# Loading w_down in sixteen 8-partition transfers in a streaming decode kernel

## The chip, the core and the metric

The kernel runs on one core of a Trainium2 chip. The metric is the device time of one execution in microseconds, taken as the median over several executions; less is better. The profile shown here is one further execution, recorded by the hardware profiler.

## What is computed

One decode step of a gated mix of two branches, for one token x of width 512. Branch A is grouped-query attention over a cache of 32768 positions (32 query heads, 8 key/value heads, head width 128) with its query and output projections. Branch B is a SwiGLU feed-forward layer of width 1792. A sigmoid gate mixes them.

```python
def _A_ref(x, k_cache, v_cache, wq, wo):
    q = (x @ wq).reshape(B, Sq, Hq, Dh).transpose(0, 2, 1, 3)
    k = jnp.repeat(k_cache, rep, axis=1)
    v = jnp.repeat(v_cache, rep, axis=1)
    p = _softmax(jnp.einsum("bhqd,bhkd->bhqk", q, k) * (Dh ** -0.5))
    o = jnp.einsum("bhqk,bhkd->bhqd", p, v)
    return o.transpose(0, 2, 1, 3).reshape(B, Sq, Hq * Dh) @ wo

def _B_ref(x, w_gate, w_up, w_down):
    return (_silu(x @ w_gate) * (x @ w_up)) @ w_down

g = _sigmoid((x * gate_w).sum(-1, keepdims=True))
return g * _A_ref(...) + (1 - g) * _B_ref(...)
```

All inputs are bfloat16. The two caches are 64 MB each; the weights wq, w_gate, w_up, w_down and wo come to about 14 MB. Every byte is read once.

## The kernel before

**The stream.** A list named `stream` (L65 to L71) has 35 entries, numbered 0 to 34, and gives the order of all large loads: "Q" (wq), two K entries of group 0, "F" (w_gate and w_up), then K of group g and V of group g-1 in turn for both halves of the cache, the last two V entries, and "O" (wo). A K or V entry is half of one group's cache, 16384 positions: 128 partitions of 32768 bytes, 4 MB. Each partition holds 128 consecutive positions.

**Pages.** SBUF holds five pages of 4 MB (`page`, NPG = 5). Entry i uses page i mod 5. Besides these there is a buffer of its own for w_down: `wd`, 128 partitions of 14 x 512 bfloat16, 14336 bytes in each partition.

**The queue that issues.** SyncE (SP) walks through the stream (L259 to L288). For entry i of 5 or more it first waits until TensorE has released entry i-5 (L261), then it issues the transfer. So at most five entries are issued and not yet released. w_gate, w_up and, right behind them, w_down are issued with entry 3 ("F", L268 to L274). wo is cut into five transfers along its rows (`WO_CUTS`, L276 to L279). All these transfers go through one DMA queue, q1, which the sixteen DMA engines serve; every transfer adds 16 to its semaphore when it has landed. ScalarE issues only the two small loads of x and gate_w (L463, L464).

**What uses the data.** TensorE takes the entries in the same order (L428 to L442). For a K entry it transposes 128 blocks (`emit_fill`, L346), VectorE copies them to SBUF (L578), and TensorE forms the scores (L364). For a V entry it waits for the exponentials of ScalarE and accumulates `ps_o` (L386). Right before entry 32, the V entry of group 7 and half 0, `emit_ffn_out` (L412) waits for w_down and multiplies with it. After the last V entry come the normalisation, the products with wo in five parts as these land (L451 to L454), a transpose of the result and the store of 4 x 128 elements (L290).

The lines that the change touches are L269 to L274 (the "F" branch of SP's loop) and L414 (the wait for w_down).

Of the kernel before, what the change touches and what calls it, by code (L numbers as in the profile page):

```python
# [13 lines left out]
def bass_gated_mix__gqa_block_cached__swiglu_ffn__decode_kernel(  # L14
# [24 lines left out]
    FC = F // 128  # L39
# [20 lines left out]
    assert KC * H * DH <= PAGE and 2 * KC * F <= PAGE and WOJ * NOUT <= PAGE  # L60
    WO_CUTS = [0, 16, 24, 28, 30, 32]
    OC = NOUT // 128


    stream = [("Q",), ("K", 0, 0), ("K", 0, 1), ("F",)]  # L65
# [7 lines left out]
    with ExitStack() as es:  # L73
        def S_(name):
            return es.enter_context(nc.semaphore(name))
# [4 lines left out]
        sem_ld_wd = S_("s_ld_wd")  # L80
# [39 lines left out]
        def T(name, shape, dt):  # L120
            return es.enter_context(nc.sbuf_tensor(name, shape, dt))
# [23 lines left out]
        wd = T("wd", [128, FC, NOUT], BF16)  # L145
# [13 lines left out]
        O2 = T("O2", [128, WOJ], BF16)  # L159
        res_col = T("res_col", [128, OC], BF16)  # L160
        res_row = T("res_row", [OC, 128], BF16)

# [18 lines left out]
        def cache_view(i):  # L181
            return page[:, i % NPG, :].rearrange("p (r d) -> p r d", d=DH)
# [28 lines left out]
        with nc.Block("main") as block:  # L211
# [45 lines left out]
            @block.sync  # L257
            def _(sp):
                for i, e in enumerate(stream):  # L259
                    if i >= NPG:  # L260
                        sp.wait_ge(*freed[i - NPG])  # L261
                    sem = sem_page[i % NPG]
                    if e[0] == "Q":
                        sp.dma_start(wq_v, A_wq.rearrange("(p c) n -> p c n", c=KC)).then_inc(  # L264
                            sem, 16
                        )
                    elif e[0] == "F":
                        for w, src in enumerate((B_w_gate, B_w_up)):  # L268
                            sp.dma_start(  # L269
                                wgu[:, w, :, :], src.rearrange("(p c) f -> p c f", c=KC)  # L270
                            ).then_inc(sem, 16)
                        sp.dma_start(
                            wd[:, :, :], B_w_down.rearrange("(p j) n -> p j n", j=FC)
                        ).then_inc(sem_ld_wd, 16)  # L274
                    elif e[0] == "O":
                        src = A_wo.rearrange("(p j) n -> p j n", j=WOJ)  # L276
                        for k, s in enumerate(sem_wo):
                            a, b = WO_CUTS[k], WO_CUTS[k + 1]
                            sp.dma_start(wo_v[:, a:b, :], src[:, a:b, :]).then_inc(s, 16)  # L279
                    else:  # L280
                        cache = A_k_cache if e[0] == "K" else A_v_cache
                        _k, g, b = e
                        sp.dma_start(
                            cache_view(i),
                            cache[0, g, b * BLK : (b + 1) * BLK, :].rearrange(
                                "(p r) d -> p r d", r=R
                            ),
                        ).then_inc(sem, 16)  # L288
                sp.wait_ge(sem_dve_row, 1)
                sp.dma_start(  # L290
                    out[0, 0, :].rearrange("(c n) -> c n", c=OC), res_row[:, :]
                ).then_inc(sem_out, 16)
                sp.wait_ge(sem_out, 16)

            @block.tensor
            def _(pe):
# [103 lines left out]
                def emit_proj(w, vec, j, first, last):  # L400
                    for oc in range(OC):
                        ins = pe.matmul(  # L402
                            ps_c[:, oc : oc + 1],
                            w[:, j, oc * 128 : (oc + 1) * 128],
                            vec[:, j : j + 1],
                            start=first and oc == 0,
                            stop=last,
                            skip_group_check=True,
                        )
                    return ins  # L410

                def emit_ffn_out():  # L412
                    pe.wait_ge(sem_dve_tT, 1)
                    pe.wait_ge(sem_ld_wd, 16)  # L414
                    for j in range(FC):
                        emit_proj(wd, tT, j, j == 0, False)

# [10 lines left out]
                for i, e in enumerate(stream):  # L428
                    if e == ("V", G - 1, 0):
                        emit_ffn_out()  # L430
                    elif e == ("V", G - 1, NB - 1):
                        emit_sums()
                    if e[0] != "O":
                        pe.wait_ge(*landed[i])
                    if e[0] == "Q":
                        emit_q()
                    elif e[0] == "F":
                        emit_ffn()
                    elif e[0] == "K":
                        emit_k(i)  # L440
                    elif e[0] == "V":
                        emit_v(i, e[1], e[2])  # L442
# [8 lines left out]
                for k, s in enumerate(sem_wo):  # L451
# [5 lines left out]
                pe.matmul(  # L457
                    ps_r[0:OC, 0:128], res_col[:, :], ident[:, :], start=True, stop=True
                ).then_inc(sem_pe_fin, 1)
# [41 lines left out]
            def _(dve):  # L501
# [104 lines left out]
                dve.wait_ge(sem_pe_sum, 1)  # L606
                dve.tensor_copy(res_col[:, :], ps_c[:, 0:OC]).then_inc(sem_dve_res, 1)  # L607
                dve.wait_ge(sem_pe_fin, 1)
# [29 lines left out]
```

## Time and profile before

| | |
|---|---|
| time, median of 3 runs (lowest to highest) | 361.88 us (361.78 to 361.90) |
| the profiled execution's own time | 361.94 us |
| its span in the profile | 360.1 us |
| TensorE matmul, busy | 273.6 us (76% of the span) |
| VectorE, busy | 185.3 us (51%) |
| ScalarE, busy | 30.4 us (8%) |
| moved by DMA | 148.99 MB in 5972 packets, mean 414 GB/s |
| issue of w_down on SP | at 3.16 us, takes 0.45 us |
| products with w_down on TensorE | 336.4 to 337.9 us |
| five issues of wo on SP | 317.21 to 319.44 us |
| issue of the result's store on SP | at 358.50 us |

The span runs from the first to the last recorded instruction; the run's own time is 1.84 us longer. Times inside the profile count from the span's start. A line such as L283 is a line of the kernel before. A page of the profile gives busy times, the span in 40 slices, the DMA queues, the chain of work that ended last, groups of instructions, and the transfers with their times from issue to landing. Beside what is printed, the trace keeps a record of each DMA packet (start, duration, bytes, queue) and of each step of a semaphore that a landing transfer raises, so that a transfer on sixteen engines leaves sixteen landing times.

### The profile page before, as it was taken

What the parts mean: (1) busy time and instruction counts of PE and PEld (TensorE: products, weight loads), DVE (VectorE), ACT (ScalarE), POOL (GpSimd) and SP (SyncE); (2) the same over time, 40 slices, a digit from 0 to 9 for tenths busy, and PEclk for the clock granted to TensorE, in tenths of its full rate; (3) what the DMA queues carried; (4) which work ended last, traced back from release to release, by engine and by line L of the source; (5) the groups of instructions that cost most, each with busy time, mean ns of one, the idle gap of its engine ahead of it and who ended that gap; (6) DMA issues with size and microseconds to landing.
All of it is one profiled execution on the core that took longest, in us unless ns stands there. A gap on an engine that the chain in (4) does not pass through costs nothing.

```text
span 360.1 us, 14005 instructions
## 1 busy us (share of the span) xinstructions
PE 273.6 (76%) x6580; PEld 269.4 (75%) x6580; DVE 185.3 (51%) x305; ACT 30.4 (8%) x142; POOL 4.6 (1%) x19
## 2 busy tenths in 40 slices
PE   0339988958696968969796969799696959697474
PEld 0339988958696968969796969799596859697474
DVE  0218935829292845738291937557282917566001
ACT  1000001500400030000300030001200030001100
POOL 0000000000000000000000000000000000000000
PEclk9999976959587785959695877859596956878555
DMA  8999999999999999999999999999999999999972
GB/s 335 422 439 402 441 422 435 431 419 435 424 426 442 421 415 439 424 433 428 414 440 424 420 442 417 422 439 419 439 428 420 435 424 420 440 420 430 423 302 101
DMA packets 5972, 148.99 MB, mean 414 GB/s; under 512 B 666, under 2 KB 668, under 8 KB 1052
## 3 DMA queue, kind: packets, MB, share of 16 engines
q1 hardware_dynamic: 5912, 148.12, 96.4%
q8 instruction: 51, 0.84, 0.9%
q14 instruction: 5, 0.04, 0.0%
q10 hardware_dynamic: 4, 0.00, 0.0%
HBM read 148.11 MB, written 0.00 MB: 411 GB/s over the span
## 4 chain that ended last, share of the span: by engine, by line
DMA 51%; PE 40%; issue 7%; SPq 1%; another core or an unknown queue 0%; DVE 0%
DMA page<-in_A_k_cache_dram 40%; PE pst L346 24%; DMA page<-in_A_wo_dram 11%; PE ps_sc L364 8%; PE ps_o L386 7%; PE ps_m L329 2%; SPq L279 0%; PE pst L402 0%; SPq L264 0%; PE pst L457 0%; DVE res_row L609 0%; DVE res_col L607 0%
## 5 line engine op out<-in xcount | busy, mean ns | idle before, releaser
L578 DVE COPY ktT<-pst 128x1024 bf16<-128x1024 bf16 x256 | 168.7, 691 | 119.0 <-PE pst L346 118.7
L346 PE MATMUL pst<-ident,page 128*128 128x128 bf16 x2048 | 179.3, 245 | 18.4 <-DMA page<-in_A_k_cache_dram 16.1
L346 PEld LDWEIGHTS pst<-ident,page 128*128 128x128 bf16 x2048 | 143.6, 111 | 19.8 <-issue 10.0
L386 PE MATMUL ps_o<-ET,page 128*128 128x4 bf16 x2048 | 65.0, 168 | 44.6 <-issue 42.2
L364 PE MATMUL ps_sc<-qT,ktT 128*128 128x4 bf16 x2048 | 90.2, 165 | 5.7 <-issue 5.1
L386 PEld LDWEIGHTS ps_o<-ET,page 128*128 128x128 bf16 x2048 | 59.7, 100 | 45.9 <-issue 43.3
L364 PEld LDWEIGHTS ps_sc<-qT,ktT 128*128 128x128 bf16 x2048 | 80.2, 98 | 6.6 <-issue 5.7
L476 ACT ACTIVATE nbias<-gmax 128x4 f32<-128x4 f32 x8 | 1.6, 206 | 279.9 <-POOL gmax L253 279.9
L486 ACT ACTIVATE ET<-ps_sc,nbias 128x128 bf16<-128x128 f32 x64 | 22.5, 377 | 0.4 <-ACT nbias L476 0.2
L566 DVE TENSOR_REDUCE pmaxf<-ps_sc 128x4 f32<-128x512 f32 x16 | 11.0, 690 | 13.3 <-PE ps_sc L364 13.3
L486 ACT ACTIVATION_READ_ACCUMULATOR ET<-ps_sc,nbias 128x1 f32 x64 | 13.8, 216 | 0.0
L315 PE MATMUL ps_m<-xT,page 128*128 128x1 bf16 x128 | 3.6, 165 | 5.3 <-DMA page<-in_A_wq_dram 5.3
L315 PEld LDWEIGHTS ps_m<-xT,page 128*128 128x128 bf16 x128 | 3.5, 104 | 5.4 <-issue 5.4
L329 PE MATMUL ps_m<-xT,page 128*128 128x1 bf16 x112 | 6.9, 198 | 0.0
L253 POOL PARTITION_ALL_REDUCE gmax<-pmax x8 | 3.0, 374 | 303.3 <-DVE pmax L570 303.3
L329 PEld LDWEIGHTS ps_m<-xT,page 128*128 128x128 bf16 x112 | 6.8, 168 | 0.0
L302 PE MATMUL ps_m<-ones_bf,x_row 1*128 1x1 bf16 x4 | 0.3, 171 | 7.8 <-DMA gw_row<-in_gate_w_dram 7.8
L302 PEld LDWEIGHTS ps_m<-ones_bf,x_row 1*128 1x128 bf16 x4 | 0.2, 112 | 7.8 <-DMA gw_row<-in_gate_w_dram 7.8
L594 DVE RECIPROCAL rS<-pst 128x32 f32<-128x32 f32 x1 | 0.4, 358 | 10.1 <-PE pst L420 10.1
L402 PE MATMUL pst<-O,page 128*128 128x1 bf16 x128 | 4.0, 166 | 1.8 <-issue 1.1
L402 PEld LDWEIGHTS pst<-O,page 128*128 128x128 bf16 x128 | 3.7, 105 | 2.1 <-issue 1.2
L503 DVE CAST xT<-ps_m 128x4 bf16<-128x4 f32 x1 | 0.2, 161 | 8.3 <-PE ps_m L302 8.3
(48 smaller groups left out, 18.5 us busy)
## 6 DMA issues: line engine op xcount, KB each, us to landing
page<-in_A_k_cache_dram SPq DMA_DIRECT2D x16, 4096.0 KB, 40.1
page<-in_A_v_cache_dram SPq DMA_DIRECT2D x16, 4096.0 KB, 37.9
page<-in_A_wq_dram SPq DMA_DIRECT2D x1, 4096.0 KB, 12.7
page<-in_A_wo_dram SPq DMA_DIRECT2D x1, 2048.0 KB, 34.9
page<-in_B_w_gate_dram SPq DMA_DIRECT2D x1, 1792.0 KB, 35.9
page<-in_B_w_up_dram SPq DMA_DIRECT2D x1, 1792.0 KB, 39.7
wd<-in_B_w_down_dram SPq DMA_DIRECT2D x1, 1792.0 KB, 43.5
page<-in_A_wo_dram SPq DMA_DIRECT2D x1, 1024.0 KB, 37.1
```

The costliest lines, as they stand in the source:

```text
L253: pool.partition_all_reduce(gmax[:, g, :], pmax[:, g, :], 128, ReduceOp.max).then_inc(sem_gmax, 1)
L302: ins = pe.matmul(ps_m[:, base + c : base + c + 1], srcv[:, c, :], ones_bf[0:1, 0:1], start=True, stop=True,)
L315: ins = pe.matmul(ps_m[:, M_Q0 + h : M_Q0 + h + 1], wq_v[:, c, h * DH : (h + 1) * DH], xT[:, c : c + 1], start=(c == 0), stop=(c == KC - 1),)
L329: ins = pe.matmul(ps_m[:, base + j : base + j + 1], wgu[:, w, c, :].rearrange("d (p j) -> d j p", j=FC)[:, j, :], xT[:, c : c + 1], start= ...
L346: ins = pe.transpose(pst[j % NST][:, t * 128 : (t + 1) * 128], view[:, q * TPF + t, :], ident[:, :],)
L364: ins = pe.matmul(ps_sc[f % NSC][:, col : col + HPG], ktT[:, j % NKT, t * 128 : (t + 1) * 128], qT[:, g * HPG : (g + 1) * HPG], start=True ...
L386: ins = pe.matmul(ps_o[:, g * HPG : (g + 1) * HPG], view[:, r, :], ET[:, g % NEG, :, n], start=(n == 0), stop=(n == NT - 1),)
L402: ins = pe.matmul(ps_c[:, oc : oc + 1], w[:, j, oc * 128 : (oc + 1) * 128], vec[:, j : j + 1], start=first and oc == 0, stop=last, skip_gr ...
L476: act.activation(nbias[:, g, :], gmax[:, g, :], ACT.Copy, scale=-SCALE).then_inc(sem_nbias, 1)
L486: act.activation(ET[:, g % NEG, h, b * R : (b + 1) * R], sc[:, h, :], ACT.Exp, bias=nbias[:, g, h : h + 1], scale=SCALE, accum_out=esum[:, ...
L566: dve.tensor_reduce(pmaxf[:, f, :], sc, AX.X, ALU.max).then_inc(sem_pmax, 1)
L578: dve.tensor_copy(ktT[:, j % NKT, :], pst[j % NST][:, :]).then_inc(sem_cp, 1)
```

## The change

w_down is no longer loaded behind w_up by one transfer. It is cut along its partitions into 16 transfers of 8 partitions each; the c-th is issued with entry 8 + c of the stream (entries 8 to 23), after SP's wait for the free page and right before that entry's own transfer. All sixteen raise the same semaphore, and the wait ahead of the products with w_down is for 256 in place of 16. Sources, destinations and the bytes that are loaded are the same.

```diff
+    WD_P = 8
+    WD_N = 128 // WD_P
+    WD_AT = 8
...
                     sem = sem_page[i % NPG]
+                    if 0 <= i - WD_AT < WD_N:
+                        p = (i - WD_AT) * WD_P
+                        sp.dma_start(
+                            wd[p : p + WD_P, :, :],
+                            B_w_down.rearrange("(p j) n -> p j n", j=FC)[p : p + WD_P, :, :],
+                        ).then_inc(sem_ld_wd, 16)
...
-                        sp.dma_start(
-                            wd[:, :, :], B_w_down.rearrange("(p j) n -> p j n", j=FC)
-                        ).then_inc(sem_ld_wd, 16)
...
-                    pe.wait_ge(sem_ld_wd, 16)
+                    pe.wait_ge(sem_ld_wd, 16 * WD_N)
```

## The prediction

> **What bounds the kernel now.** I read the page's slices first, to see which resource is full and where it stops being full.
>
> ```profile
> PE   0339988958696968969796969799696959697474
> DMA  8999999999999999999999999999999999999972
> GB/s 335 422 439 402 441 422 435 431 419 435 424 426 442 421 415 439 424 433 428 414 440 424 420 442 417 422 439 419 439 428 420 435 424 420 440 420 430 423 302 101
> ```
>
> DMA is full in every slice from the second to the 38th, at about 428 GB/s, while TensorE has gaps nearly everywhere. The two last slices, 9 us each, run at 302 and 101 GB/s. The chain of work that ended last names TensorE for much of the span, but only because SP's issues wait for released pages:
>
> ```profile
> DMA 51%; PE 40%; issue 7%; SPq 1%; another core or an unknown queue 0%; DVE 0%
> ...
> page<-in_A_k_cache_dram SPq DMA_DIRECT2D x16, 4096.0 KB, 40.1
> page<-in_A_v_cache_dram SPq DMA_DIRECT2D x16, 4096.0 KB, 37.9
> ...
> wd<-in_B_w_down_dram SPq DMA_DIRECT2D x1, 1792.0 KB, 43.5
> ```
>
> A 4 MB page at 428 GB/s needs 9.8 us, yet lands 38 to 40 us after its issue: it stands behind three other pages. A later issue costs nothing as long as that queue holds some 28 us of work. So the end is set by the DMA engines emptying the queue. Then the queues, and the end of the stream in windows (the last three columns are granted clock, DMA share and GB/s):
>
> ```profile
> DMA packets 5972, 148.99 MB, mean 414 GB/s; under 512 B 666, under 2 KB 668, under 8 KB 1052
> ...
> q1 hardware_dynamic: 5912, 148.12, 96.4%
> q8 instruction: 51, 0.84, 0.9%
> ...
> q10 hardware_dynamic: 4, 0.00, 0.0%
> ```
>
> ```profile
> 340.00:345.00 5.00, 3.37 (x107) 3.28 (x106) 0.00 (x0) 0.00 (x0) 0.00 (x0) 0.50 0.98 411
> 345.00:350.00 5.00, 2.59 (x96) 2.55 (x96) 0.60 (x2) 0.00 (x0) 0.00 (x0) 0.50 0.69 282
> 350.00:355.00 5.00, 2.82 (x93) 2.58 (x91) 0.60 (x3) 0.00 (x0) 0.00 (x0) 0.50 0.50 200
> 355.00:360.10 5.10, 2.64 (x82) 2.29 (x78) 0.44 (x2) 0.00 (x0) 0.00 (x0) 0.50 0.07 24
> ```
>
> The share falls to exactly one half: eight of sixteen engines are done while eight still work. The landing records say it engine by engine: the last part of wo lands on six engines at 346.2 to 347.2 us, on a seventh at 348.2, on an eighth at 351.2, and on the other eight at 355.5 to 357.2. For the first transfer, wq, the sixteen lay within 0.9 us. The gap grows evenly: some engine falls back by about 1.56 us whenever it serves a packet of q8, and the packet records show 48 of the 51 packets going round eight engines, six to each (6 x 1.56 = 9.4 us). I call these the late eight and the others the early eight. TensorE's last products start at 357.26 us, right behind the last of the late eight.
>
> **The change, part by part.** q1's packets took 96.4% of 16 x 360.1 us, 5554 engine-us for 148.12 MB: 26.7 KB per us and engine, so a row of w_down (14336 B) takes 0.54 us.
>
> *Removed:* one transfer of 128 rows, 8 rows for each engine: 8 x 0.54 = 4.3 us off all sixteen. The issues agree: w_up lands at 2.67 + 39.7 = 42.4 us, w_down at 3.16 + 43.5 = 46.7.
>
> *Moved earlier:* entry 4 and what follows land up to 4.3 us sooner until entry 8. It is worth nothing at the end, since the same bytes still go through the queue; the products with w_down at 336.4 us stand some 80 us behind the last piece.
>
> *Added on SP:* 15 more issues. With the neighbouring rows at 0.33 us (a page) and 0.45 (w_down), each delays its entry by at most 0.45 us, hidden by the 28 us of queue; without that cover it would be 16 x 0.45 = 7.2 us. No new wait is queued: the pieces stand behind a wait that SP had anyway.
>
> *Added on the engines.* On how many engines does a transfer of 8 partitions run? The counts tell: 41 transfers of 128 partitions with one semaphore packet from each of 16 engines are 41 x 144 = 5904 of q1's 5912 packets; 8 are left for the result's store, whose four rows thus had four semaphore packets, not sixteen: four engines. q10 has 4 packets for two loads of one row: one engine each. So a piece of 8 rows runs on eight engines, one row each. If they are the same eight each time, these carry 16 rows in place of 8 and the others none. Which eight? The packet records let me follow the engine that carried x: it never serves a q8 packet and ends with the early eight. So I take it that short transfers start from the early ones. [...]
>
> By rows alone, the late eight then gain 4.3 us (357.2 to 352.9), the early ones lose 4.3 plus 15 more semaphore packets of 9 ns (0.1 us): the eighth of them ends at 351.2 + 4.4 = 355.6, which is the new end: 357.2 - 355.6 = 1.6 us won. That is the lower bound of the cost.
>
> *What the rows of before do not show* is eight engines writing into eight neighbouring partitions at once. In a 128-row transfer each engine has eight rows of its own. From below: the rows don't disturb each other, 0.54 us for a piece. From above: eight rows never went in faster than one engine wrote them, 8 x 0.54 = 4.3 us for a piece, 3.8 us more, 16 x 3.8 = 60 us. Nearest is the one place where two packets meet on one path, a q8 packet and a page packet on one engine: the visit costs 1.56 us where its 16 KB alone would be 0.61, so a meeting costs 0.95 us. Several engines meet here, but they come at slightly different times (the early ones are spread over 2 us), so I take one such meeting for each row: 0.54 + 0.95 = 1.49 us for a piece.
>
> [...]
>
> *The sum.* Early engines: 16 x 1.49 + 0.1 - 4.3 = 19.6 us more. Six of them had 10.0 to 11.0 us of lead over the end and the seventh 9.0; the seventh ends last of them, 19.6 - 9.0 = 10.6 us behind the old end. The eighth had 6.0, but runs 3 to 5 us out of step with the others by then; at half the meetings it ends at 12.0 - 6.0 = 6.0 us. So +10.6 us on the profiled execution's own 361.94 us: 372.5 us. Its time stands 0.06 us over the median, so the same holds for the median. What follows the last landing (0.38 us of products, the copy, the transpose, the store) is unchanged.
>
> **The rivals.** *No disturbance.* The rows go in freely: 361.9 - 1.6 = 360.3 us, faster. For it: the early eight idle for up to 11 us at the end and the late eight give up 4.3. Against it: nothing in the trace shows eight rows side by side going in freely. It decides as long as the disturbance stays under 1.6 / 16 = 0.10 us for a piece on the eighth engine; the other seven could stand (9.0 - 4.4) / 16 = 0.29 us before they reach the old end.
>
> *Other eight engines, free rows.* If the eight that serve the pieces include some of the late ones (the record of x fixes only one), those end 4.4 us later: 366.3 us.
>
> *Other eight engines, with disturbance.* The late ones among them get the whole 19.6 us without a lead: 381.5 us.
>
> *The pieces run on sixteen engines after all*, half a row each. Then nothing is shifted, the same bytes go through evenly, and the time stays at 361.9 us. The store's packet count speaks against it.
>
> **How the numbers follow.** My forecast, early engines with disturbance, 372.5 us: 0.52. No disturbance, 360.3: 0.25. Other engines, free: 0.06. Other engines, disturbed: 0.10. Sixteen engines, no change: 0.07. Two differences of 0.2% (0.7 us) or less can't be told apart in a measurement of this kernel, so faster 0.25, same 0.07, slower 0.68. With 1.0 us for a piece the same sum gives 364.7, with 2.0 us 380.7: the forecast's own range. The range that takes in the rival on the other side and leaves out most of the disturbed other engines is 359.5 to 380.0.
>
> **What would show it.** q1 should have 5912 - 16 + 128 = 6024 packets: if more, the pieces ran on more engines. The windows at the end tell which group is late: half the share again if one group still waits for the other. The landing records of pages 8 to 23 tell the size: the late eight fall back by 1.56 us in 52 us, 0.29 us for a page, so with my forecast the early ones lose 1.49 - 0.29 = 1.2 us a page against them, close up and then fall behind; if free, the gap shrinks by 0.25 us a page. Rows of 14336 B should last longer than 0.54 us, by about 0.95. The products of TensorE on the last part of wo must start right behind the last landing, as before. My number is wrong if the pieces' rows keep their 0.54 us; my reading is wrong if the end is no longer the DMA's.

## The result, and the profile after

The kernel with the change takes 388.21 us (median of 4 runs, 387.9 to 390.1) against 361.89 us before: 1.0719 times as long, 95% interval 1.0659 to 1.0779. It is slower, as forecast, but by 26.3 us and not by 10.6, and the range given (to 380.0) does not hold it. The profiled execution took 390.1 us, its span is 388.3 us; the sums below are made against that one.

The page of the kernel after, its slices and its queues:

```profile
DMA  8999999999999999999999999999999999999940
GB/s 324 432 430 420 436 430 432 427 375 359 378 397 393 379 378 383 377 372 402 359 348 377 362 375 382 358 382 416 429 427 423 430 432 424 430 425 426 378 201 38
DMA packets 6084, 148.99 MB, mean 384 GB/s; under 512 B 778, under 2 KB 780, under 8 KB 1164
...
q1 hardware_dynamic: 6024, 148.12, 95.3%
```

The queue q1 has 6024 packets, the number the prediction named for pieces on eight engines. The engines are busy in every slice as before, yet from the 9th to the 27th slice (9.7 us each) they move 348 to 402 GB/s instead of some 428. The same in windows (us, then busy time and count of each engine, granted clock, DMA share, GB/s):

```profile
68.00:78.00 10.00, 5.00 (x167) 4.84 (x165) 1.93 (x6) 0.00 (x0) 0.00 (x0) 0.61 0.99 424
78.00:264.00 186.00, 129.82 (x3069) 127.54 (x3066) 91.08 (x140) 13.70 (x69) 1.48 (x4) 0.72 1.01 376
264.00:345.00 81.00, 63.88 (x1538) 63.09 (x1539) 45.40 (x70) 6.20 (x34) 0.74 (x2) 0.75 1.00 427
```

The pieces are in flight from 79 to 264 us. In just that time a full DMA share (1.01) moves 376 GB/s; before the first piece and after the last it is 424 and 427. (1 - 376/427) x 186 us is 22 us lost. Nobody waits more: the packets themselves take longer, a page packet 1.39 us on average from 78 to 264 us against 1.22 in the kernel before. The landing records say on which engines. For some entries of the stream, the landing on the first and on the last of the sixteen engines (us):

```
entry       before           after          difference
          first   last     first   last     first   last
  4        54.6   56.6      50.3   52.3      -4.2   -4.3
  7        83.7   87.0      79.5   83.2      -4.2   -3.7
 11       122.6  125.9     123.2  130.2      +0.6   +4.3
 15       161.4  166.3     165.9  178.9      +4.5  +12.6
 19       200.3  206.7     210.9  227.4     +10.6  +20.7
 24       248.8  256.8     266.8  285.0     +17.9  +28.2
 33       336.3  347.4     354.2  375.5     +17.9  +28.1
last wo   346.2  357.2     364.1  385.5     +17.9  +28.3
```

Entries 4 to 7 land some 4.2 us sooner, w_down being out of the way. From entry 7 to 24 even the first landing falls back by 22.1 us, 1.38 us for each piece, and the engine that lands first carries no row of w_down at all (e7 below shows which engines carry rows). The last landing falls back by 32 us. After entry 24 nothing changes any more.

The end of the stream in windows, and TensorE's last products with wo:

```profile
360.00:365.00 5.00, 2.41 (x91) 2.41 (x91) 0.19 (x1) 2.98 (x17) 0.00 (x0) 0.54 0.91 383
365.00:370.00 5.00, 2.24 (x79) 2.09 (x77) 0.00 (x0) 0.00 (x0) 0.00 (x0) 0.50 0.87 363
370.00:375.00 5.00, 2.45 (x77) 2.31 (x73) 0.60 (x2) 0.00 (x0) 0.00 (x0) 0.50 0.60 242
375.00:380.00 5.00, 3.78 (x129) 3.59 (x129) 0.41 (x2) 0.00 (x0) 0.00 (x0) 0.50 0.23 91
380.00:385.00 5.00, 3.56 (x116) 3.34 (x117) 0.19 (x1) 0.00 (x0) 0.00 (x0) 0.50 0.14 51
```

```profile
385.51 0.37 PE L409 MATMUL pst<-O,page 128*128 128x1 bf16 x8 [0.26 <-DMA page<-in_A_wo_dram]
```

Before, the share stood at one half for the last stretch: eight engines against eight. Now it runs out in steps, 0.60, 0.23, 0.14: from 380 us on some two engines out of sixteen still work, 0.14 x 16 = 2.2. TensorE still starts right behind the last landing, so the DMA still sets the end.

### The profile page after: what moved, and what is told of

It reads as the page before. It is cut to its first block, busy times and chain, and to the rows that moved or that the text cites. A ratio compares the mean times of both kernels' runs of the same rounds, so it can differ in the third digit from the quotient of the medians.

```text
span 388.3 us, 14020 instructions
## 1 busy us (share of the span) xinstructions
PE 274.1 (71%) x6580; PEld 269.4 (69%) x6580; DVE 185.4 (48%) x305; ACT 30.3 (8%) x142; POOL 4.5 (1%) x19
## 3 DMA queue, kind: packets, MB, share of 16 engines
q1 hardware_dynamic: 6024, 148.12, 95.3%
## 4 chain that ended last, share of the span: by engine, by line
DMA 51%; PE 37%; issue 9%; another core or an unknown queue 1%; SPq 1%; DVE 0%
DMA page<-in_A_k_cache_dram 29%; PE pst L353 21%; DMA page<-in_A_v_cache_dram 12%; DMA page<-in_A_wo_dram 10%; PE ps_sc L371 7%; PE ps_o L393 7%; PE ps_m L336 2%; SPq L286 0%; DVE ktT L585 0%; SPq L269 0%; PE pst L409 0%; SPq L274 0%; PE pst L464 0%; DVE res_row L616 0%
```

## The experiments

Two words for what follows. Sixteen engines carry a transfer of 128 partitions (w_down of before landed on them at 44.9 to 46.6 us), eight rows each. The partitions that an engine writes in such a transfer I call its own; a row that it writes elsewhere I call foreign. No record holds a partition, so which eight they are is an estimate from the runs below. Pieces of eight rows at every fourth partition of 0 to 63 go in without loss (429 GB/s in the first half of e1, 428 in e7). The engines that carry such a piece I number by its rows, 0 to 7, and call them the lowest eight, and engine 0, on which the single rows of e10 fall, the lowest: names alone, as no record numbers an engine. By the estimate engine i owns partitions 4i to 4i + 3 and 32 + 4i to 35 + 4i. Rows from 64 on are foreign to these eight (378 GB/s in the second half of e1); how the other eight engines share those partitions, no run shows. In a piece of the change, where row i of eight goes to engine i, nearly all rows are foreign: 120 of 128 in all.

**Source or destination (e1 to e3).** The first changes both sides of the pieces, the second the source alone, the third the destination alone.

```diff
-                        p = (i - WD_AT) * WD_P
+                        c = i - WD_AT
+                        p = 32 * (c // 4) + c % 4
...
-                            wd[p : p + WD_P, :, :],
-                            B_w_down.rearrange("(p j) n -> p j n", j=FC)[p : p + WD_P, :, :],
+                            wd[p : p + 29 : 4, :, :],
+                            B_w_down.rearrange("(p j) n -> p j n", j=FC)[p : p + 29 : 4, :, :],
```

> Sixteen pieces of 8 rows as in the change, but each piece takes every fourth partition of a group of 32 (0, 4, ... 28, then 1, 5, ... 29, and so on) in source and destination. Theory D (destination): eight neighbouring partitions share few ways into SBUF, the writers jam there and hold up all sixteen engines; spread out they do not, so the time is the sum without disturbance, 360.3 us (359.5 to 361.5), and page packets stay at 1.21 us. Theory S (source): eight engines reading one closed 112 KB stretch of DRAM at once is what jams; the rows now lie 57 KB apart, so also about 360. Theory K (a transfer on eight engines as such, with its semaphores and its place between pages): about 388, as the change.

> As the change in the destination (eight neighbouring partitions a piece), but each piece reads every fourth row of a group of 32 rows of w_down, so the rows of w_down stand in other partitions than the product expects. Theory D: about 388 us, page packets up to 2 us and more during each piece. Theory S: about 360 us. Theory K: about 388.

> The mirror image: each piece reads eight neighbouring rows of w_down (112 KB in one stretch) as in the change, but writes them to every fourth partition of a group of 32, so the rows of w_down stand in other partitions than the product expects. Theory D: about 360 us. Theory S: about 388. Theory K: about 388.

Measured: 376.02 us for both sides (six runs; ratio 1.036, interval 1.0318 to 1.0401), 388.87 for the source alone, 376.06 for the destination alone (one run each). The source plays no part. The destination does, but spreading it wins only half, which none of the three theories had said. The windows of e1 show why: its first eight pieces go to partitions 0 to 63 (78 to 158 us), its last eight to 64 to 127:

```profile
78.00:158.00 80.00, 63.54 (x1528) 62.80 (x1526) 44.64 (x69) 7.49 (x35) 0.74 (x2) 0.76 1.01 429
158.00:250.00 92.00, 62.83 (x1532) 61.61 (x1530) 44.64 (x70) 6.21 (x34) 0.74 (x2) 0.72 1.00 378
```

For the first half the pieces cost nothing at all, 429 GB/s; for the second half as much as in the change, 378. With the destination alone spread (e3) the two halves look the same, and with the source alone (e2) the whole stretch is slow:

```profile
78.00:158.00 80.00, 60.71 (x1504) 59.63 (x1501) 43.38 (x69) 7.50 (x35) 0.74 (x2) 0.77 1.00 428
158.00:250.00 92.00, 63.82 (x1529) 62.63 (x1527) 44.88 (x69) 6.22 (x34) 0.74 (x2) 0.72 1.00 379
```

```profile
78.00:264.00 186.00, 125.42 (x3040) 123.08 (x3038) 88.40 (x137) 13.70 (x69) 1.48 (x4) 0.73 1.01 379
```

The packet records of e1 agree: in the first half the rows last 0.54 us and page packets (one 32 KB row each) are as short as ever, 1.215 us; in the second, page packets take 15 to 23 us longer in each stretch of 10 us, summed over all engines. By this the rows of the first half are each engine's own and those of the second half all foreign, though they stand as far apart. So a crowd in one place is not needed: theory D, as I had put it, falls too. The first engine to land, which carries no piece, loses 10.9 us from entry 15 to 24, 1.36 us for each of the eight foreign pieces, just as in the change.

Following each engine's packets in e1 showed something else: of the eight engines that carry pieces, two also serve instruction packets of q8. The late eight are not the eight without pieces.

**The move alone (e4).** w_down in one transfer of 128 partitions ahead of entry 8.

```diff
-    WD_P = 8
+    WD_P = 128
```

> The move alone: w_down in one transfer of 128 partitions, issued ahead of entry 8 of the stream instead of behind w_up. All theories: no change, 361.9 us (361.2 to 362.6), since the same bytes go evenly through the sixteen engines and the late eight stay as late as they were. If the move itself costs, it shows here.

Measured 362.05 us (ten runs), ratio 1.0004, interval 0.9973 to 1.0034. The move costs nothing.

**Sixteen probes in one kernel (e5).** The kernel before, with one extra little transfer ahead of each of sixteen entries.

```diff
+                    if i == 8:
+                        sp.wait_ge(sem_ld_wd, 16)
+                    if 0 <= i - 8 < len(SMP):
+                        if i >= 13:
+                            sp.wait_ge(sem_smp[i - 13], 16)
+                        n = FC * NOUT - 16 * (i - 7)
+                        sp.dma_start(
+                            wd[:, :, :].rearrange("p j n -> p (j n)")[SMP[i - 8], 0:n],
+                            B_w_down.rearrange("(p j) n -> p (j n)", j=FC)[SMP[i - 8], 0:n],
+                        ).then_inc(sem_smp[i - 8], 16)
```

> The kernel before, w_down loaded as there; on top, sixteen different probes are issued ahead of entries 8 to 23, each loading a few rows of w_down once more into their own place (row lengths 14304 B down to 13824 B, 32 B less each, so that the packet records tell them apart). In order: 8 rows at every fourth partition from 0; 8 neighbouring from 40; 8 at every fourth from 64; one row at 34; one at 5; one at 65; 4 neighbouring from 0; 8 at every eighth from 4; 4 at every fourth from 35; 16 neighbouring from 96; 7 at every fourth from 33; 6 at every fourth from 1; 2 at every fourth from 2; 8 at every fourth from 34; 8 at every 16th from 7; 16 at every eighth from 4. Measured: how much longer than 1.216 us the page packets of the next 10 us take, summed over all engines (0.7 to 1.5 us where nothing disturbs; 15 to 22 in the change). Theory M (mismatch: an engine that writes into partitions which another engine writes in full transfers holds up all sixteen, however few rows): every probe away from its engine's own partitions costs, even the single rows at 5 and 65 (some 3 us or more); own ones (0, 34, 35, 33, 1, 2 steps of four) cost nothing. Theory J (jam: only several writers at once into one group of partitions cost): the single rows and the 8 at every fourth from 64 stay near 1 to 3 us; 4 and 8 and 16 neighbouring ones cost 8 us or more.

What the packet records gave, in the order of the probes; the last column is the time that page packets took above 1.216 us, summed over all engines from the probe to the next one:

```
rows, partitions                 foreign   mean row   sum over
                                 rows      us         page packets, us
8 at 0, 4 .. 28                    0       0.54        1.3
8 at 40 .. 47                      7       0.77       18.8
8 at 64, 68 .. 92                  8       0.67       20.3
1 at 34                            0       0.54        1.2
1 at 5                             1       0.53        3.5
1 at 65                            1       0.53        2.4
4 at 0 .. 3                        3       0.63        6.8
8 at 4, 12 .. 60                   7       0.63       15.3
4 at 35, 39 .. 47                  0       0.53        0.6
16 at 96 .. 111                  >=8       0.79       44.3
7 at 33, 37 .. 57                  0       0.53        0.7
6 at 1, 5 .. 21                    0       0.53        2.0
2 at 2, 6                          0       0.52        0.6
8 at 34, 38 .. 62                  0       0.52        0.7
8 at 7, 23 .. 119                  8       0.58        8.0
16 at 4, 12 .. 124               >=4       0.62       20.4
```

Two stretches of 10 us around a probe in windows, first eight foreign rows (104 us), then eight own ones (219 us):

```profile
104.00:114.00 10.00, 8.05 (x208) 7.98 (x206) 7.62 (x12) 0.00 (x0) 0.00 (x0) 0.99 1.00 370
219.00:229.00 10.00, 5.94 (x171) 5.79 (x169) 2.11 (x4) 3.11 (x17) 0.37 (x1) 0.56 1.01 432
```

Every probe without a foreign row stays at 0.6 to 2.0 us, what instruction packets cause in the kernel before as well; every probe with foreign rows is above that, the single row at 65 barely (2.4; e10 settles single rows). Theory M holds, and the price is some 2 to 3 us of engine time, summed over the sixteen engines, for a foreign row of 14 KB (18.8 over 7, 20.3 over 8, 15.3 over 7). For the two probes of sixteen rows the table has the least number of foreign rows that the estimate above gives, as what the other eight engines own is not shown. The last probe but one comes out at 1.0; the rows of the last two were spread over 8 and 13 us, since the engines were no longer in step, and part of what they cost lies behind the window. Such rows themselves take up to 0.26 us longer than own ones on average, and no longer when alone (0.53): page packets pay most of it.

**Pieces of sixteen (e6).**

```diff
-    WD_P = 8
+    WD_P = 16
```

> As the change, with 8 pieces of 16 neighbouring partitions in place of 16 pieces of 8, so that all sixteen engines carry one row of each piece and no engine gets more bytes than before. If the loss of the change is the uneven load alone: 361.9 us. If it is the disturbance (M or J) at 1.4 us for each piece and engine whatever the rows: 8 x 1.4 = 11 us, 373 us. If it goes with the rows (0.18 us of delay on every engine for each foreign row): 128 rows in both, about 385 us.

Measured 384.96 us (one run). No engine gets more bytes than before, yet 23 us are lost, and 26.3 in the change: it goes with the number of rows (128 again, at least 80 of them foreign by the same estimate, in 8 pieces), not with the number of pieces, and it needs no uneven load. In the windows the eight pieces (74 to 176 us) take the rate down to 346 GB/s:

```profile
74.00:176.00 102.00, 65.55 (x1569) 64.28 (x1570) 45.23 (x70) 7.50 (x35) 0.74 (x2) 0.72 1.01 346
180.00:340.00 160.00, 125.91 (x3014) 124.05 (x3012) 88.72 (x136) 12.45 (x68) 1.49 (x4) 0.76 1.00 428
```

Not all of the 23 us is the DMA's. The last part of wo lands at 376.9 us on the last engine, 19.7 us later than before, but TensorE runs all its products with wo behind that:

```profile
377.18 3.57 PE L409 MATMUL pst<-O,page 128*128 128x1 bf16 x128 [0.29 <-DVE O L612]
```

TensorE was behind the DMA by then, and the end is some 3.4 us later than the landing alone would have made it. Why is not settled; the profiled execution of e4 shows the same without any disturbance: it took 366.65 us, the longest of its ten, with the last landing at 357.4 us. The 19.7 us still speak for the rows: at 1.4 us for a piece it would have been 11.

**Uneven load without foreign rows (e7).** The kernel before, loading the rows of partitions 0 to 63 once more, all own.

```diff
+                    if i == 8:
+                        sp.wait_ge(sem_ld_wd, 16)
+                    if 8 <= i < 16:
+                        p = 32 * ((i - 8) // 4) + i % 4
+                        sp.dma_start(
+                            wd[p : p + 29 : 4, :, :],
+                            B_w_down.rearrange("(p j) n -> p j n", j=FC)[p : p + 29 : 4, :, :],
+                        ).then_inc(sem_again, 16)
```

> The kernel before, w_down loaded as there, and 8 more pieces of 8 rows ahead of entries 8 to 15 that load the rows of partitions 0 to 63 once more, each piece at every fourth partition, so that each engine writes only its own partitions. The bytes rise by 0.9 MB, all on the lowest eight engines: 8 x 0.54 = 4.3 us for each of them, nothing for the others, no disturbance. If the lowest eight are the eight that end early (as the prediction took it), the eighth ends at 351.2 + 4.3 and the time stays at 361.9 us. If two of the late ones are among them (as the packet records of the first experiment show), the latest ends 4.3 us later: 366.2 us.

Measured 364.79 us (ten runs), ratio 1.0076, interval 1.005 to 1.0102. The rate in the middle is untouched, and only the end is longer:

```profile
80.00:160.00 80.00, 62.72 (x1523) 61.75 (x1521) 43.77 (x69) 7.50 (x35) 0.74 (x2) 0.78 1.00 428
...
350.00:355.00 5.00, 3.94 (x129) 3.67 (x129) 0.60 (x3) 0.00 (x0) 0.00 (x0) 0.50 0.63 254
355.00:362.90 7.90, 4.14 (x129) 3.73 (x129) 0.44 (x2) 0.00 (x0) 0.00 (x0) 0.50 0.11 42
```

Two of the eight engines with pieces serve q8, and these two land last, at 360.0 us. They are of those that landed at 355.5 to 355.9 before; with 4.3 us more they end 2.8 us behind the old end of 357.2 us, and the time rose by 2.7 to 2.8. I had expected 4.3 by taking them for the very latest. The other six end at 350.7 to 355.5: had all eight been early ones, the time would not have moved by this. The two earliest engines still land at 346.5 us: they carry no piece.

**All pieces at once (e8).** The 16 pieces of the change issued together behind w_up.

```diff
-                    if 0 <= i - WD_AT < WD_N:
...
+                        for p in range(0, 128, WD_P):
+                            sp.dma_start(
+                                wd[p : p + WD_P, :, :],
+                                B_w_down.rearrange("(p j) n -> p j n", j=FC)[p : p + WD_P, :, :],
+                            ).then_inc(sem_ld_wd, 16)
```

> The 16 pieces of 8 neighbouring partitions all issued together behind w_up, where the one transfer of before stood, instead of one ahead of each of entries 8 to 23. If what costs is each foreign row by itself (some 2.5 engine-us for each of 120 rows, spread over sixteen engines, plus 4.3 us of own rows on a late engine): about 388 us, as the change, with the loss in one place. If it is the mixing with page packets (each row meeting packets of engines that are elsewhere in the stream): less, since the eight engines then write w_down side by side, perhaps 370 to 380. If spreading them out were what costs: 361.9 to 366.

Measured 378.16 us (one run).

```profile
40.00:50.00 10.00, 5.54 (x135) 5.36 (x132) 6.45 (x11) 0.00 (x0) 0.00 (x0) 1.00 1.07 264
50.00:60.00 10.00, 7.42 (x128) 7.34 (x128) 0.69 (x1) 0.00 (x0) 0.00 (x0) 0.59 1.01 167
...
80.00:160.00 80.00, 61.61 (x1508) 60.74 (x1506) 44.45 (x73) 11.11 (x50) 0.74 (x2) 0.74 1.00 428
```

For 20 us the sixteen engines, all busy, move 264 and 167 GB/s; from 70 us on nothing is lost any more. An engine without rows lands its last part of wo at 353.5 us: 353.5 - 346.2 + 4.3 = 11.6 us of delay, 0.73 us for a piece, half of the 1.38 in the change. So spreading the pieces between the pages made them dearer by some 10 us, and a foreign row has no fixed price: had each cost the same wherever it stands, it would have been 388. Here the rows themselves pay more, 1.15 us on average against 0.76 in the change, and the page packets less, 98 us in sum above 1.216 us each. Why is not shown; that scattered rows meet page packets of engines elsewhere in the stream is only what the expectation supposed.

**Cut along the columns (e9).** Seven transfers of 128 partitions, two column blocks each, ahead of entries 8 to 14.

```diff
+    WD_J = FC // 7
+    WD_N = 7
...
+                        j = (i - WD_AT) * WD_J
+                        sp.dma_start(
+                            wd[:, j : j + WD_J, :],
+                            B_w_down.rearrange("(p j) n -> p j n", j=FC)[:, j : j + WD_J, :],
+                        ).then_inc(sem_ld_wd, 16)
```

> w_down in 7 transfers, each of all 128 partitions and 2 of its 14 column blocks (2 KB a row), ahead of entries 8 to 14. Many transfers spread over the middle of the stream, but every engine writes its own partitions and all get the same bytes. If the mismatch is what costs: 361.9 us, at most 0.5 us more for the shorter rows. If many transfers between the pages cost by themselves: clearly more, some 5 to 12 us.

Measured 362.23 us (ten runs), ratio 0.9995, interval 0.9975 to 1.0015. While the seven are in flight (the first stretch) the rate is 424 GB/s, after them 428:

```profile
70.00:150.00 80.00, 63.21 (x1520) 62.54 (x1516) 45.64 (x73) 7.49 (x35) 0.74 (x2) 0.79 1.00 424
150.00:250.00 100.00, 78.78 (x1876) 77.51 (x1872) 56.24 (x86) 6.21 (x34) 0.74 (x2) 0.74 1.00 428
```

Seven transfers in the middle of the stream cost nothing that can be told from no change, as long as every engine writes its own partitions.

**Single rows (e10).** The probes again, one row each, all on the lowest engine.

> The kernel before with sixteen probes of a single row each ahead of entries 8 to 23, all carried by one engine, the lowest: partitions 0, 4, 33, 64, 8, 68, 1, 100, 16, 124, 2, 28, 72, 34, 44, 92. That engine's own partitions are 0 to 3 and 32 to 35, so 0, 33, 1, 2 and 34 are own, eleven are foreign. Theory M: page packets take 1 to 3 us longer in sum after each foreign row, spread over all engines, and nothing after an own one. Theory J (a jam of several writers): nothing after any, 0.7 to 1.3 us as everywhere. Time within 2 us of before either way.

Sum over page packets in the 4 us around each row:

```
own:      0: 0.08   33: 0.08   1: 0.64   2: 0.54   34: 0.09
foreign:  4: 1.33   64: 1.56   8: 3.01   68: 2.20   100: 0.81   16: 2.38
          124: 2.09   28: 2.38   72: 1.82   44: 1.30   92: 2.07
```

The two own rows above 0.1 have an instruction packet beside them (a page packet of 1.76 and of 1.69 us; without it 0.06 and 0.09). The foreign ones average 1.90 us against 0.29 for the own ones: 1.6 us of engine time for one foreign row with nothing else foreign in flight. The first landing of wo falls back by 1.1 us, which is 11 x 1.6 / 16. In e5, around the row at 5, the records show how it is made up: the next packet of the engine that carried it takes 1.55 us instead of 1.22, one other packet 1.69, and some twelve more 1.31 us each, a tenth of a microsecond too long. In e10 each of the eleven foreign rows has two long packets (1.44 to 1.70 us; three at 92), but only eight of them have the slightly longer ones, 11 or more; at 4, 44 and 100 there is at most one. Why these three differ is not known. Theory J falls, M stands.

The time was 365.69 us (one run), more than the 2 us I had allowed. The lowest engine, which lands early in the kernel before, now lands last, at 359.5 us, 2.3 us behind the old end; 16 rows of 0.53 us and the long packet behind each foreign one fall on it alone. The rest is TensorE, behind the DMA at the end as in e6: its products with wo run until 361.26 us, 1.8 us behind that landing.

```profile
357.69 3.57 PE L431 MATMUL pst<-O,page 128*128 128x1 bf16 x128 [0.29 <-DVE O L636]
```

No version was found that beats the kernel before. To relieve the late engines, others would have to write those engines' partitions, and these are foreign rows; a layout of w_down on fewer partitions was not tried.

## Why the prediction was right and wrong

**The bound** was read rightly. The DMA queue sets the end in both kernels, and the last products start right behind the last landing.

**What is removed and moved** came out as worked out: 4.2 us sooner for entries 4 to 7 (4.3 predicted), nothing at the end from the move (e4), and nothing that can be told from six more issues on SP (e9).

**Eight engines for each piece, one row each,** was right: 6024 packets on q1. That they are the same eight each time, which the sum takes for granted, fits the ends of the runs: in e7 the two earliest engines do not move (346.5 us), and in the change two land by 364.6 us, all others from 372.1 us on.

**"So I take it that short transfers start from the early ones"** was wrong in part. The record of x fixed one engine, the lowest, and I took the other seven to be of its kind. Two of the lowest eight serve instruction packets and are late. In e7 the lowest eight carry eight rows more than before, as in the change, with no disturbance at all, and this alone made the kernel 2.7 us slower. So the rival on the other side, 360.3 us, could not have come true; nor could 366.3, as these two are not the very latest. Of the rivals, 381.5 us (late engines among the eight, with disturbance) came nearest; it allowed for late engines, but had the same price as the forecast.

**"I take one such meeting for each row: 0.54 + 0.95 = 1.49 us for a piece"** is the step that failed. That the pieces disturb the stream was right. But they need not meet each other: a single row costs too, and eight spread ones as much as eight neighbours. And I put the price on the eight engines that carry the rows, where a lead of 9 us would absorb half of it. The rows themselves last 0.76 us on average, not 1.49. The larger part of what they cost falls on the page packets of all sixteen engines: while the pieces were in flight these took 352 us above 1.216 us each, in sum; less the 15 that instruction packets cause in such a stretch, that is 2.8 us for each of the 120 foreign rows, and 1.38 us for a piece on an engine that carries nothing. A lead of one engine over another pays for nothing when both are held up. Nor was the upper bound (3.8 us more for a piece) one for this: it bounded the time of the carrying engine.

The sum with what the runs showed: a late engine among the lowest eight landed at 355.6 us; less 4.3 for the removed transfer, plus 16 x (0.54 + 1.38) = 30.7, plus 0.1, is 382.1 us; the last landing was measured at 385.5. The missing 3.4 us are the size of what this sum leaves out, that the rows last 0.76 us and not 0.54: 16 x 0.22 = 3.5 us. By that the carrying engines are held up on their page packets about as long as the others.

**What decides the price** is not how close the writers stand: eight foreign rows at every fourth partition cost as much (20.3 us, the third probe of e5) as eight neighbours (18.8), and a single foreign row costs too (1.6 us, e10). It is whether an engine writes its own partitions: by this the sixteen rows of e10 and the sixteen probes of e5 sort rightly.

**What would show it:** the test by landing records was the useful one. It said that with my forecast the first and the last landing would close up first; instead they drew apart from the first piece on and both fell behind, and this pointed to all engines being held up. My sign of being wrong, rows that keep their 0.54 us, could not have told this: what was wrong showed on other packets.

## What to carry to other kernels

In a kernel bound by its loads, look at the landing times engine by engine, not at the mean rate: here half of the engines were done 6 to 11 us before the last one, but a lead read there is worth something only against a cost that falls on those engines alone. When a load has to be cut, cut it along the free dimension and leave all 128 partitions in every transfer (362.23 us here), not along the partitions (388.21); if a transfer must take fewer partitions, check whether each of its engines stays on the partitions that it writes in full transfers (429 GB/s for pieces at every fourth partition of 0 to 63 in e1, 376 for neighbours in the change). A transfer on few engines is not a transfer on idle engines: measure which engines those are before relying on them (in e7 two of the eight were late ones, and the kernel was 2.7 us slower).

## What the runs showed of the hardware

A row of 14 KB that an engine writes into partitions of another engine holds up other engines' packets too: 1.6 us of engine time on average when it is alone (e10, where eight rows of eleven held up eleven or more other packets slightly and three little more than two packets), 2 to 3 us when several are in flight (e5). Written into its own partitions it costs nothing beyond its 0.54 us (0.06 to 0.09 us on all the others, e10). The DMA share does not show it: it is 1.01 while the rate falls from 428 to 346 GB/s (e6). Where the engines meet was not found, and no run wrote a foreign row while the engine that owns the place stood idle. And in the kernel before, the instruction packets of q8, 16 KB each, cost an engine 1.56 us a visit, 48 of the 51 go round eight of the sixteen engines, and these eight end last (355.5 to 357.2 us, the others by 351.2).
